# One-head TensorE loop body with branch arms, and query projections with x as the stationary column, in a decode-attention kernel

## The chip, the cores and the metric

The kernel runs on one core of one Trainium2 chip. The metric is the device time of one execution in microseconds (us); lower is better. "Before" was run beside every experiment on the same chip; its medians lie between 1328.2 and 1328.3 us throughout.

## The reference

Two attention layers for one new token, A and B, each with its own inputs; the two results are put side by side.

```python
# A: 32 heads, 32768 keys each        B: 32 query heads on 8 K/V heads, last 4096 keys
q = (x @ wq).reshape(B, Sq, H, Dh).transpose(0, 2, 1, 3)        # x is (1, 1, 512), Dh = 128
scores = jnp.einsum("bhqd,bhkd->bhqk", q, k_cache) * (Dh ** -0.5)
p = softmax(scores)
o = jnp.einsum("bhqk,bhkd->bhqd", p, v_cache)
out = o.transpose(0, 2, 1, 3).reshape(B, Sq, H * Dh) @ wo
```

All of it is bf16. There is one query, so each byte of K and V is used once: A alone reads 32 heads of 8 MB of K and 8 MB of V.

## The kernel before

Every operation is recorded first, with its dependencies; then each engine's list is emitted, with semaphore waits. TensorE and VectorE emit the A heads as a hardware loop, since their instructions repeat. The synchronizing engine (SP) issues the loads. K arrives with keys on the partitions, so TensorE transposes it (256 transposes of 128x128 a head), VectorE copies each eight of them from PSUM, and then the score matmuls run.

K has a buffer of three thirds, each half a head. Even heads lie in thirds 1 and 0, odd heads in 1 and 2. So the second half's addresses differ between even and odd heads, and the loop body holds two heads:

```python
def k_thirds(self, g):
    return (1, 0) if g % 2 == 0 else (1, 2)
...
for g in range(NQH):                                   # the A heads
    self.loop = {"pe": g // 2, "dve": g // 2}          # two heads are one iteration
    self.load_k(g, 1 if g < NQH - 1 else 2)            # 8 MB; waits until both thirds are free
    self.load_v(g)                                     # 8 MB; waits for the last value product
    self.emit_qcopy(g)
    self.emit_unit("A", g)                             # transposes, copies, scores
    self.emit_stats("A", g)
    self.emit_PT("A", g)
    self.emit_PV("A", g)                               # value product: 64 matmuls of 512 columns
...
with e.Fori(0, nit):
    for o, w in zip(its[-1], plans[-1]):
        run(e, o, [(sems[name], rel) for name, rel in w])
    for name, sem in sems.items():
        e.sem_inc(sem, -step[name])._wait_ge(sem, step[name])
```

The query projection uses each 128x128 block of wq as the stationary operand and one column of x as the moving one:

```python
for tt in range(4):
    for h in range(NQH):
        inst = e.matmul(ps[:, h:h + 1], lhsT=wq[:, 4096 * tt + 128 * h:4096 * tt + 128 * h + 128],
                        rhs=t["x"][:, tt:tt + 1], start=(tt == 0 and h == 0), stop=(tt == 3),
                        skip_group_check=True)
```

Of the kernel before, what the change touches and what calls it, by code (L numbers as in the profile page):

```python
# [9 lines left out]
DH = 128  # L10
NQH = 32
# [24 lines left out]
class Op:  # L36
# [2 lines left out]



    __slots__ = ("eng", "fn", "deps", "loop", "pos", "to", "users", "before")

    def __init__(self, eng, fn, deps, to, loop):
        self.eng = eng
        self.fn = fn
        self.deps = [d for d in deps if d is not None]
        self.to = to
        self.loop = loop
        self.users = []  # L50


class _Kernel:
# [30 lines left out]



    def op(self, eng, fn, *deps, to=None):
        o = Op(eng, fn, deps, to, self.loop.get(eng))
        self.prog[eng].append(o)
        return o  # L90

# [80 lines left out]
    def emit(self, eng):  # L172
        ops = self.prog[eng]
        nit = len({o.loop for o in ops} - {None})
        its = [[o for o in ops if o.loop == k] for k in range(nit)]
        first = next((i for i, o in enumerate(ops) if o.loop is not None), len(ops))
        pre, post = ops[:first], ops[first + sum(map(len, its)):]

        def run(e, o, waits):
            for sem, val in waits:  # L180
                e.wait_ge(sem, val)
            inst = o.fn(e)
            if o.to:
                inst.then_inc(self.sem(eng, o.to), 1)

        def straight(e, part, seen, base):
            for o in part:
                waits = []
                for name, (sem, val) in self.needs(o).items():
                    if val > seen.get(name, 0):  # L190
                        seen[name] = val
                        waits.append((sem, val - base.get(name, 0)))
                run(e, o, waits)

        def body(e):
            seen, base = {}, {}
            straight(e, pre, seen, base)
            if not nit:
                return

            assert len(set(map(len, its))) == 1
            need = [[self.needs(o) for o in it] for it in its]
            top = lambda k, name: max(n[name][1] for n in need[k] if name in n)
            sems = {name: sem for it in need[-2:] for n in it for name, (sem, _) in n.items()}
            step = {name: top(-1, name) - top(-2, name) for name in sems}
            for name in [x for x in sems if not step[x]]:
                if top(0, name) > seen.get(name, 0):
                    e.wait_ge(sems[name], top(0, name))
                    seen[name] = top(0, name)
                del sems[name]  # L210
            start = {name: top(-2, name) - step[name] * (nit - 1) for name in sems}
            plans = []
            for k, it in enumerate(need):
                cur, plan = {}, []
                for n in it:
                    w = []
                    for name, (sem, val) in n.items():
                        if name not in sems:
                            continue
                        rel = val - start[name] - step[name] * k  # L220
                        if rel > cur.get(name, 0):
                            cur[name] = rel
                            w.append((name, rel))
                    plan.append(sorted(w))
                plans.append(plan)
            for k, plan in enumerate(plans):
                for p, q in zip(plan, plans[-1]):
                    assert p == q or (k == 0 and set(p) <= set(q)), (eng, k, p, q)
            for name, sem in sems.items():
                if start[name] > 0:  # L230
                    e.sem_inc(sem, -start[name])._wait_ge(sem, start[name])
                elif start[name] < 0:
                    e.sem_inc(sem, -start[name])
            with e.Fori(0, nit):
                for o, w in zip(its[-1], plans[-1]):
                    run(e, o, [(sems[name], rel) for name, rel in w])
                for name, sem in sems.items():
                    e.sem_inc(sem, -step[name])._wait_ge(sem, step[name])
            for name in sems:
                base[name] = seen[name] = start[name] + step[name] * nit  # L240
            straight(e, post, seen, base)

        return body

    def alloc(self):
# [19 lines left out]
        for name, d in self.X.items():  # L265
            HG = d["HG"]
            self.c[name] = dict(
                x=sb(f"x_{name}", [128, 4], BF16),
                oc=[sb(f"oc_{name}{i}", [128, DH + 1], F32) for i in range(2)],
                b=sb(f"b_{name}", [128, 32], F32),  # L270
                cm=sb(f"cm_{name}", [128, 32], F32),
                mr=sb(f"mr_{name}", [1, HG], F32),
# [8 lines left out]

        self.qz = sb("qz", [128, 32 * self.X["B"]["NKVH"] + 64], BF16)
        self.qa = sb("qa", [128, NQH], BF16)
        self.qw = sb("qw", [128, 64], BF16)
        self.hw = sb("hw", [128, 32], F32)
        ps = nc.alloc_psum_tensor
# [38 lines left out]

    def k_thirds(self, g):
        return (1, 0) if g % 2 == 0 else (1, 2)

    def load_k(self, g, parts):
        w = HALF * DH  # L330
# [36 lines left out]
    def plan(self):  # L367
# [4 lines left out]
        self.copies = []  # L372
        self.pending = []
        self.psread = self.ptread = self.sread = self.accread = None
        self.gath = self.qcopy = self.hcopy = None
        self.constants()
        a, b = self.X["A"], self.X["B"]

# [15 lines left out]
        self.emit_spread("B")  # L394

        for g in range(NQH):
            self.loop = {"pe": g // 2, "dve": g // 2}
            self.load_k(g, 1 if g < NQH - 1 else 2)
            self.load_v(g)
            self.emit_qcopy(g)  # L400
# [17 lines left out]
    def constants(self):  # L418
# [15 lines left out]
        self.k_hw = pool(lambda g: g.memset(self.hw[:, :], 0.0))  # L434
        dve = lambda fn, *deps, **k: self.op("dve", fn, *deps, **k)
        dve(lambda v: v.memset(self.G[:, :], 0.0))
        self.accread = dve(lambda v: v.memset(self.ACC[:, :], 0.0))
        for n in ("B", "A"):
            self.op("act", lambda e, n=n: e.dma_start(
# [18 lines left out]
                             self.k_pool)  # L458

    def emit_qproj(self, name):  # L460
        t = self.c[name]
        slot = self.WQ_SLOT[name]
        ps, wq = self.ACC, self.vbuf[:, HALF * DH * slot:HALF * DH * (slot + 1)]
        def mm(e):
            inst = None
            for tt in range(4):
                for h in range(NQH):
                    inst = e.matmul(ps[:, h:h + 1], lhsT=wq[:, 4096 * tt + 128 * h:4096 * tt + 128 * h + 128],
                                    rhs=t["x"][:, tt:tt + 1], start=(tt == 0 and h == 0), stop=(tt == 3),
                                    skip_group_check=True)  # L470
            return inst
        o = self.op("pe", mm, (self.xsem[name], 16), self.landed("v", slot), self.accread, to="dve")
        self.free["v"][slot] = o
        if name == "B":
            o = self.op("dve", lambda v: v.tensor_copy(
                self.qz[:, 32:].rearrange("p (k w) -> p k w", w=32)[:, 0:8, 0:4],
                ps[:, 0:NQH].rearrange("p (k a) -> p k a", a=4)), o, self.k_pool)
            self.qb = o
        else:
            o = self.op("dve", lambda v: v.tensor_copy(self.qa[:, :], ps[:, 0:NQH]), o)  # L480
            self.qready = o
        self.accread = o

    def emit_qcopy(self, g):
        self.qcopy = self.op("act", lambda s: s.activation(
# [2 lines left out]
    def emit_unit(self, name, g, hooks={}):  # L488
# [4 lines left out]
        order = [(t, i, 8 * (t - lo) + st) for i, t in enumerate(thirds) for st in range(8)]  # L493
        for n, (t, i, st) in enumerate(order):
            for half in range(2):
                self.emit_T(HALF * lo + 16 * st + 8 * half, self.landed("k", g if name == "B" else i), t)
            if n % 2:
                if n // 2 in hooks:
                    hooks[n // 2]()
# [1 line left out]
                if len(self.pending) > 1:  # L501
                    self.emit_S(self.pending.pop(0))

    def emit_T(self, tile, landed, third):
        b = self.nbatch
        self.nbatch += 1
        T, KT = self.T[b % NT][:, :].bitcast(BF16), self.kt[b % NKT]
        src = self.kbuf[:, DH * tile:DH * tile + 1024]
        def tr(e):
            inst = None  # L510
            for k in range(8):
                inst = e.transpose(T[:, 128 * k:128 * k + 128], src[:, DH * k:DH * k + DH], self.ident[:, :])  # L512
            return inst
        o = self.op("pe", tr, landed, self.copies[b - NT] if b >= NT else self.k_ident, to="dve")
        self.copies.append(self.op("dve", lambda v: v.tensor_copy(KT[:, :], T[:, :]), o, to="pe"))  # L515
        self.free["k"][third] = o

# [24 lines left out]
    def emit_stats(self, name, g):  # L542
# [2 lines left out]
        d, t = self.X[name], self.c[name]  # L545
        KC, HG = d["KC"], d["HG"]
        W = KC * HG
        k = g % 2
        tr, m4 = self.tr, self.m4
        dve = lambda fn, *deps, **k: self.op("dve", fn, *deps, **k)  # L550
        o = dve(lambda v: v.reduce_max(tr["in"][:, 0:1], self.S[:, :], axis=AXX), self.sdone, self.k_pool,  # L551
# [1 line left out]
        if name == "A":  # L553
# [7 lines left out]
            o = dve(lambda v: v.tensor_copy(t["nb"][:, k:k + 1], self.ACC[:, 64:65]), o, to="act")  # L561
            self.sread = self.op("act", lambda s: s.activation(  # L562
                out=self.psb[:, :], in_=self.S[:, :], func=ACTF.Exp, bias=t["nb"][:, k:k + 1], scale=self.SCALE,
                accum_out=t["oc"][k][:, DH:DH + 1]), o, self.psread, to="pe")
            return
        o = dve(lambda v: v.transpose(tr["a"][:, :], tr["in"][:, :]), o)
        for c in range(STRIPS):
# [27 lines left out]
    def emit_PV(self, name, g):  # L595
# [23 lines left out]
            self.free["v"][i] = pv  # L619

        pv = self.emit_gather(name, g, DH, DH + 1)
        oc = t["oc"][g % 2][:, 0:DH]
        o = None
        for j in range(4):
            src, hot = acc[:, DH * j:DH * j + DH], t["hot"][:, j:j + 1]
# [11 lines left out]
    def emit_gather(self, name, g, c, c2):  # L637
# [1 line left out]
        t, HG, c0 = self.c[name], self.X[name]["HG"], self.GCOL[name]  # L639
        win = self.hw[:, :] if name == "A" else t["hsel"][:, 32 - HG * g:64 - HG * g]  # L640
        return self.op("pe", lambda e: e.matmul(  # L641
            self.G[0:32, c0 + c:c0 + c2], lhsT=win, rhs=t["oc"][g % 2][:, c:c2], start=False, stop=True,
            skip_group_check=True), self.accread, self.sread, self.hcopy if name == "A" else self.k_sel, to="dve")

    def emit_spread(self, name):
# [79 lines left out]
```

## Time and profile before

| | before |
|---|---|
| time, median of 6 runs | 1328.32 us (1328.13 to 1328.79) |
| DMA, 100 to 1280 us | all 16 engines busy, 433 GB/s |
| TensorE / VectorE busy | 73% / 57% |
| TensorE's wait for K | 156.2 us in 31 waits, 5.0 us each |
| one A head | 38.50 us (mean of heads 5 to 30, between first transposes) |
| TensorE words in the loop body | 1,579, by count in the program |

From the page of the kernel before: busy time by engine, the DMA share and rate in 40 slices of the span, and the data and instruction queues (packets, megabytes, share of the 16 engines' time).

```profile
span 1326.3 us, 28821 instructions
PE 972.0 (73%) x13436; PEld 681.1 (51%) x13436; DVE 749.4 (57%) x1345; ACT 54.8 (4%) x167; POOL 2.3 (0%) x17
...
DMA  9999999999999999999999999999999999999998
GB/s 403 440 425 428 436 437 431 435 433 433 433 425 439 437 433 429 441 431 427 439 433 427 439 441 429 427 441 433 425 439 439 429 431 441 429 429 439 433 427 349
...
q1 hardware_dynamic: 13048, 570.44, 99.6%
q8 instruction: 12, 0.20, 0.1%
```

The DMA engines are at 9 in every slice but the last. A 9 means only "90% or more", so it is worth asking for a stretch by itself. The windows view of the kernel before gives for 100 to 1280 us: busy time of PE, PEld, DVE, ACT and POOL, then the granted clock, the DMA share and GB/s.

```profile
100.00:1280.00 1180.00, 881.21 (x12045) 615.12 (x12043) 676.40 (x1186) 49.16 (x155) 0.00 (x0) 0.83 1.00 433
```

DMA share 1.00 at 433 GB/s; over the whole span the page has 570.43 MB read from HBM, 430 GB/s.

How much room is there behind the DMA? The timeline of the kernel before, cut to one head: an SPq line is the issue of a load, the PE line the first transposes of the next head, with the idle time before them and what ended it.

```profile
250.26 0.33 SPq L303 DMA_DIRECT2D kbuf<-in_A_k_cache_dram  x1
...
271.80 0.33 SPq L303 DMA_DIRECT2D vbuf<-in_A_v_cache_dram  x1
...
277.83 5.34 PE L512 MATMUL psT<-ident,kbuf 128*128 128x128 bf16 x64 [4.01 <-DMA kbuf<-in_A_k_cache_dram]
```

V is issued at 271.80 us, 6 us before the K ahead of it has landed, so the engines always have the next load in the queue. And TensorE itself idles for K in each head. A slower TensorE thus has two cushions: its own wait, and the depth of the queue.

The projections in the timeline of the kernel before (start, length):

```profile
13.35 3.58 PE L468 MATMUL psACC<-x_B,vbuf 128*128 128x1 bf16 x128 [13.35 <-DMA x_B<-in_B_x_dram]
16.96 0.19 DVE L475 CAST qz<-psACC 128x32 bf16<-128x32 f32 x1 [11.50 <-PE psACC L468]
...
35.21 3.35 PE L468 MATMUL psACC<-x_A,vbuf 128*128 128x1 bf16 x128
...
38.60 0.19 DVE L480 CAST qa<-psACC 128x32 bf16<-128x32 f32 x1 [2.69 <-PE psACC L468]
```

### The profile page before, as it was taken

What the parts mean: (1) busy time and instruction counts of PE and PEld (TensorE: products, weight loads), DVE (VectorE), ACT (ScalarE), POOL (GpSimd) and SP (SyncE); (2) the same over time, 40 slices, a digit from 0 to 9 for tenths busy, and PEclk for the clock granted to TensorE, in tenths of its full rate; (3) what the DMA queues carried; (4) which work ended last, traced back from release to release, by engine and by line L of the source; (5) the groups of instructions that cost most, each with busy time, mean ns of one, the idle gap of its engine ahead of it and who ended that gap; (6) DMA issues with size and microseconds to landing.
All of it is one profiled execution on the core that took longest, in us unless ns stands there. A gap on an engine that the chain in (4) does not pass through costs nothing.

```text
span 1326.3 us, 28821 instructions
## 1 busy us (share of the span) xinstructions
PE 972.0 (73%) x13436; PEld 681.1 (51%) x13436; DVE 749.4 (57%) x1345; ACT 54.8 (4%) x167; POOL 2.3 (0%) x17
## 2 busy tenths in 40 slices
PE   3757678787677878767787866778786677878686
PEld 3544446554444655444465544446554444655453
DVE  3655456664555666455566645556664555666473
ACT  0000000000000000000000000000000000000000
POOL 0000000000000000000000000000000000000000
PEclk9767788887878888787888878788887878888798
DMA  9999999999999999999999999999999999999998
GB/s 403 440 425 428 436 437 431 435 433 433 433 425 439 437 433 429 441 431 427 439 433 427 439 441 429 427 441 433 425 439 439 429 431 441 429 429 439 433 427 349
DMA packets 13351, 570.66 MB, mean 430 GB/s; under 512 B 1812, under 2 KB 1816, under 8 KB 2200
## 3 DMA queue, kind: packets, MB, share of 16 engines
q1 hardware_dynamic: 13048, 570.44, 99.6%
q8 instruction: 12, 0.20, 0.1%
q10 hardware_dynamic: 288, 0.00, 0.0%
q14 instruction: 3, 0.02, 0.0%
HBM read 570.43 MB, written 0.00 MB: 430 GB/s over the span
## 4 chain that ended last, share of the span: by engine, by line
DMA 70%; PE 27%; DVE 1%; issue 0%; SPq 0%; ACT 0%
DMA kbuf<-in_A_k_cache_dram 65%; PE psT L512 23%; PE psS L534 4%; DMA kbuf<-in_B_k_cache_dram 3%; DMA kbuf<-in_A_wo_dram 3%; DVE kt L515 1%; PE psACC L614 0%; SPq L303 0%; DVE oc_A L630 0%; ACT psb L562 0%; DVE tr_in L551 0%; PE psPT L586 0%; ACT ptsb L589 0%; PE psPT L676 0%; PE psG L641 0%
## 5 line engine op out<-in xcount | busy, mean ns | idle before, releaser
L515 DVE COPY kt<-psT 128x1024 bf16<-128x1024 bf16 x1056 | 654.7, 684 | 236.3 <-PE psT L512 234.9
L512 PE MATMUL psT<-ident,kbuf 128*128 128x128 bf16 x8448 | 578.7, 234 | 167.5 <-DMA kbuf<-in_A_k_cache_dram 156.2
L512 PEld LDWEIGHTS psT<-ident,kbuf 128*128 128x128 bf16 x8448 | 539.2, 106 | 259.7 <-DMA kbuf<-in_A_k_cache_dram 164.3
L614 PE MATMUL psACC<-vbuf,ptsb 128*4 128x512 bf16 (+1 forms) x2112 | 190.4, 539 | 23.2 <-ACT ptsb L589 21.3
L534 PE MATMUL psS<-kt,qw 128*32 128x512 bf16 x2048 | 157.7, 385 | 15.5 <-DVE kt L515 15.5
L628 DVE TENSOR_SCALAR oc_A<-psACC,hot_A 128x128 f32<-128x128 f32 x32 | 11.2, 351 | 255.7 <-PE psG L641 255.7
L614 PEld LDWEIGHTS psACC<-vbuf,ptsb 128*4 128x4 bf16 (+1 forms) x2112 | 61.4, 113 | 142.7 <-issue 98.3
L562 ACT ACTIVATE psb<-psS,nb_A 128x512 bf16<-128x512 f32 x32 | 22.0, 687 | 1167.7 <-DVE nb_A L561 1167.7
L534 PEld LDWEIGHTS psS<-kt,qw 128*32 128x32 bf16 x2048 | 34.1, 95 | 58.0 <-DVE kt L515 31.4
L641 PE MATMUL psG<-oc_A,hw 128*32 128x128 f32 (+1 forms) x128 | 19.3, 227 | 52.3 <-DVE oc_A L630 52.3
L641 PEld LDWEIGHTS psG<-oc_A,hw 128*32 128x32 f32 x128 | 11.4, 109 | 62.4 <-DVE oc_A L630 55.0
L586 PE MATMUL psPT<-ident,psb 128*128 128x128 bf16 x136 | 18.4, 280 | 34.1 <-ACT psb L562 34.1
L630 DVE SCALAR_TENSOR_TENSOR oc_A<-psACC,hot_A,oc_A 128x128 f32<-128x128 f32 x96 | 33.7, 351 | 3.4
L551 DVE TENSOR_REDUCE tr_in<-psS 128x1 f32<-128x512 f32 x34 | 23.5, 692 | 17.3 <-PE psS L534 17.3
L586 PEld LDWEIGHTS psPT<-ident,psb 128*128 128x128 bf16 x136 | 10.4, 120 | 37.1 <-ACT psb L562 36.7
L555 PE MATMUL psACC<-rows,tr_in 128*1 128x64 f32 x64 | 8.7, 218 | 25.5 <-DVE tr_in L551 25.5
L589 ACT ACTIVATE ptsb<-psPT 128x512 bf16<-128x512 bf16 x34 | 20.3, 597 | 30.2 <-PE psPT L586 30.2
L555 PEld LDWEIGHTS psACC<-rows,tr_in 128*1 128x1 f32 x64 | 2.7, 81 | 35.1 <-DVE tr_in L551 35.1
L559 PE MATMUL psACC<-mr_A,nscale 1*128 1x1 f32 x64 | 12.1, 256 | 9.8 <-DVE mr_A L558 9.8
L559 PEld LDWEIGHTS psACC<-mr_A,nscale 1*128 1x128 f32 x64 | 9.4, 183 | 15.8 <-DVE mr_A L558 15.8
L561 DVE COPY nb_A<-psACC 128x1 f32<-128x1 f32 x32 | 5.1, 159 | 15.1 <-PE psACC L559 15.1
L558 DVE TENSOR_REDUCE mr_A<-psACC 1x1 f32<-1x64 f32 x32 | 6.8, 212 | 11.7 <-PE psACC L555 11.7
(71 smaller groups left out, 75.5 us busy)
## 6 DMA issues: line engine op xcount, KB each, us to landing
kbuf<-in_B_k_cache_dram SPq DMA_DIRECT2D x2, 4096.0 KB, 32.6
vbuf<-in_B_v_cache_dram SPq DMA_DIRECT2D x2, 4096.0 KB, 23.8
kbuf<-in_A_k_cache_dram SPq DMA_DIRECT2D x2, 4096.0 KB, 22.3
vbuf<-in_B_wq_dram SPq DMA_DIRECT2D x1, 4096.0 KB, 12.4
vbuf<-in_A_wq_dram SPq DMA_DIRECT2D x1, 4096.0 KB, 32.2
kbuf<-in_B_wo_dram SPq DMA_DIRECT2D x2, 2048.0 KB, 33.5
kbuf<-in_A_wo_dram SPq DMA_DIRECT2D x1, 1408.0 KB, 28.9
kbuf<-in_A_wo_dram SPq DMA_DIRECT2D x1, 1024.0 KB, 31.0
```

The lines of the kernel that those rows point to most:

```text
L512: inst = e.transpose(T[:, 128 * k:128 * k + 128], src[:, DH * k:DH * k + DH], self.ident[:, :])
L515: self.copies.append(self.op("dve", lambda v: v.tensor_copy(KT[:, :], T[:, :]), o, to="pe"))
L534: inst = e.matmul(self.S[32 * c:32 * c + 32, :], lhsT=win, rhs=self.kt[(bb + c // 2) % NKT][:, 512 * (c % 2):512 * (c % 2) + 512], start=b ...
L551: o = dve(lambda v: v.reduce_max(tr["in"][:, 0:1], self.S[:, :], axis=AXX), self.sdone, self.k_pool, to="pe" if name == "A" else None)
L555: o = self.op("pe", lambda e: e.matmul(self.ACC[0:1, 0:64], lhsT=tr["in"][:, 0:1], rhs=self.rows64[:, :], start=True, stop=True, skip_grou ...
L559: o = self.op("pe", lambda e: e.matmul(self.ACC[:, 64:65], lhsT=self.nscale[:, :], rhs=t["mr"][0:1, :], start=True, stop=True, skip_group_ ...
L562: self.sread = self.op("act", lambda s: s.activation(out=self.psb[:, :], in_=self.S[:, :], func=ACTF.Exp, bias=t["nb"][:, k:k + 1], scale= ...
L586: inst = e.transpose(PT[:, 128 * jj:128 * jj + 128], self.psb[:, 128 * jj:128 * jj + 128], self.ident[:, :])
L589: self.ptread = self.op("act", lambda s: s.activation(out=self.ptsb[:, :], in_=PT[:, 0:512], func=ACTF.Copy), self.psread, to="pe")
L614: inst = e.matmul(acc[32 * c:32 * c + rows, 0:512], lhsT=lhsT, rhs=rhs, start=begin, stop=end, tile_position=(0, 32 * c), skip_group_check ...
L630: o = self.op("dve", lambda v, src=src, hot=hot: v.scalar_tensor_tensor(out=oc, in0=src, scalar=hot, in1=oc, op0=ALU.mult, op1=ALU.add), p ...
L641: return self.op("pe", lambda e: e.matmul(self.G[0:32, c0 + c:c0 + c2], lhsT=win, rhs=t["oc"][g % 2][:, c:c2], start=False, stop=True, ski ...
```

## The change

Its intent: a shorter TensorE program, with one head as the loop body. What differs between even and odd heads, the addresses of the second half's transposes, goes into the two arms of a branch, four times a head. With only one accumulator left for A, the exponential also waits for the head before. The projections use x as the stationary column, 32 matmuls of 512 columns in four column strips in place of 128 of one column; the rows are then copied and turned by 8 small matmuls.

```diff
... (cut: how the loop's operations are grouped)
+            odd = None
+            if any(two for two, _ in groups):
+                assert nit % 2 == 0
+                odd = e.alloc_register(f"{eng}_odd")
+                e.reg_mov(odd, 0)
             with e.Fori(0, nit):
-                for o, w in zip(its[-1], plans[-1]):
-                    run(e, o, [(sems[name], rel) for name, rel in w])
+                for two, part in groups:
+                    if two:
+                        with e.If_eq(odd, 0):
+                            for o, w in part:
+                                run(e, o, w, o.alts[0])
+                        with e.Else():
+                            for o, w in part:
+                                run(e, o, w, o.alts[1])
+                    else:
+                        for o, w in part:
+                            run(e, o, w)
+                if odd is not None:
+                    e.reg_sub(odd, 1, odd)
                 for name, sem in sems.items():
                     e.sem_inc(sem, -step[name])._wait_ge(sem, step[name])
... (cut)
-            self.loop = {"pe": g // 2, "dve": g // 2}
+            self.loop = {"pe": g, "dve": g // 2}
... (cut: emit_qproj)
-                for h in range(NQH):
-                    inst = e.matmul(ps[:, h:h + 1], lhsT=wq[:, 4096 * tt + 128 * h:4096 * tt + 128 * h + 128],
-                                    rhs=t["x"][:, tt:tt + 1], start=(tt == 0 and h == 0), stop=(tt == 3),
-                                    skip_group_check=True)
+                for b in range(2):
+                    for c in range(STRIPS):
+                        w = 4096 * tt + 512 * (4 * b + c)
+                        inst = e.matmul(banks[b][32 * c:32 * c + 1, :], lhsT=t["x"][:, tt:tt + 1], rhs=wq[:, w:w + 512],
+                                        start=(tt == 0), stop=(tt == 3), tile_position=(0, 32 * c), skip_group_check=True)
... (cut)
+        for b in range(2):
+            o = self.op("dve", lambda v, b=b: v.tensor_copy(self.qrow[:, 512 * b:512 * b + 512], banks[b][:, :]), o)
... (cut)
+            for b in range(2):
+                for i in range(4):
+                    inst = e.matmul(ps[:, 16 * b + i:16 * b + i + 13:4], lhsT=self.qrow[:, 512 * b + 128 * i:512 * b + 128 * i + 128],
+                                    rhs=self.ident[:, 0:97:32], start=True, stop=True, skip_group_check=True)
... (cut: emit_unit)
+                if name == "A" and i == 1:
+                    alts = [HALF * min(self.k_thirds(x)) + 8 * (16 * self.last_half(x) + 2 * (st % 8) + half) for x in (0, 1)]
... (cut: A's exponential)
-                accum_out=t["oc"][k][:, DH:DH + 1]), o, self.psread, to="pe")
+                accum_out=t["oc"][k][:, DH:DH + 1]), o, self.psread, self.gath if g else None, to="pe")
```

More of the change, by code (lines that the diff above doesn't have):

```diff
@@ L36, with __init__ @@
 class Op:
-    __slots__ = ("eng", "fn", "deps", "loop", "pos", "to", "users", "before")
-    def __init__(self, eng, fn, deps, to, loop):
+    __slots__ = ("eng", "fn", "deps", "loop", "pos", "to", "users", "before", "alts")
+    def __init__(self, eng, fn, deps, to, loop, alts=None):
+        self.alts = alts
         self.eng = eng
@@ L83, in __init__, with op @@
         self.loop = {}
-    def op(self, eng, fn, *deps, to=None):
-        o = Op(eng, fn, deps, to, self.loop.get(eng))
+    def op(self, eng, fn, *deps, to=None, alts=None):
+        o = Op(eng, fn, deps, to, self.loop.get(eng), alts)
         self.prog[eng].append(o)
@@ L177, in emit, with run @@
         pre, post = ops[:first], ops[first + sum(map(len, its)):]
-        def run(e, o, waits):
+        def run(e, o, waits, fn=None):
             for sem, val in waits:
                 e.wait_ge(sem, val)
-            inst = o.fn(e)
+            inst = (fn or o.fn)(e)
             if o.to:
@@ L233, in body @@
                     e.sem_inc(sem, -start[name])
-            with e.Fori(0, nit):
-                for o, w in zip(its[-1], plans[-1]):
-                    run(e, o, [(sems[name], rel) for name, rel in w])
+            groups = []
+            for o, w in zip(its[-1], plans[-1]):
+                if not (groups and groups[-1][0] and o.alts):
+                    groups.append((bool(o.alts), []))
+                groups[-1][1].append((o, [(sems[name], rel) for name, rel in w]))
+            odd = None
[3 more added lines that the diff above has]
+                e.reg_mov(odd, 0)
+            with e.Fori(0, nit):
+                for two, part in groups:
[11 more added lines that the diff above has]
+                    e.reg_sub(odd, 1, odd)
                 for name, sem in sems.items():
@@ L268, in alloc @@
                 x=sb(f"x_{name}", [128, 4], BF16),
-                oc=[sb(f"oc_{name}{i}", [128, DH + 1], F32) for i in range(2)],
+                oc=[sb(f"oc_{name}{i}", [128, DH + 1], F32) for i in range(2 if name == "B" else 1)],
                 b=sb(f"b_{name}", [128, 32], F32),
@@ L283, in alloc @@
         self.qa = sb("qa", [128, NQH], BF16)
+        self.qrow = sb("qrow", [128, 1024], BF16)
         self.qw = sb("qw", [128, 64], BF16)
@@ L327, in k_thirds, with last_half @@
         return (1, 0) if g % 2 == 0 else (1, 2)
+    def last_half(self, g):
+        t = self.k_thirds(g)
+        return t[1] - min(t)
     def load_k(self, g, parts):
@@ L374, in plan @@
         self.psread = self.ptread = self.sread = self.accread = None
-        self.gath = self.qcopy = self.hcopy = None
+        self.gath = self.qcopy = self.hcopy = self.qread = None
         self.constants()
@@ L436, in constants @@
         dve(lambda v: v.memset(self.G[:, :], 0.0))
+        dve(lambda v: v.memset(self.PT[:, :], 0.0))
         self.accread = dve(lambda v: v.memset(self.ACC[:, :], 0.0))
@@ L462, in emit_qproj @@
         slot = self.WQ_SLOT[name]
-        ps, wq = self.ACC, self.vbuf[:, HALF * DH * slot:HALF * DH * (slot + 1)]
+        wq = self.vbuf[:, HALF * DH * slot:HALF * DH * (slot + 1)]
+        banks = (self.ACC, self.PT)
         def mm(e):
@@ L466, in mm, with turn @@
             for tt in range(4):
-                for h in range(NQH):
-                    inst = e.matmul(ps[:, h:h + 1], lhsT=wq[:, 4096 * tt + 128 * h:4096 * tt + 128 * h + 128],
-                                    rhs=t["x"][:, tt:tt + 1], start=(tt == 0 and h == 0), stop=(tt == 3),
-                                    skip_group_check=True)
+                for b in range(2):
[3 more added lines that the diff above has]
+                                        start=(tt == 0), stop=(tt == 3), tile_position=(0, 32 * c), skip_group_check=True)
             return inst
-        o = self.op("pe", mm, (self.xsem[name], 16), self.landed("v", slot), self.accread, to="dve")
+        o = self.op("pe", mm, (self.xsem[name], 16), self.landed("v", slot), self.accread, self.qread, to="dve")
         self.free["v"][slot] = o
+        for b in range(2):
+            o = self.op("dve", lambda v, b=b: v.tensor_copy(self.qrow[:, 512 * b:512 * b + 512], banks[b][:, :]), o)
+        self.accread = o
+        ps = self.G[:, 400:432]
+        def turn(e):
+            inst = None
+            for b in range(2):
+                for i in range(4):
+                    inst = e.matmul(ps[:, 16 * b + i:16 * b + i + 13:4], lhsT=self.qrow[:, 512 * b + 128 * i:512 * b + 128 * i + 128],
+                                    rhs=self.ident[:, 0:97:32], start=True, stop=True, skip_group_check=True)
+            return inst
+        o = self.op("pe", turn, o, self.qread, self.k_ident, to="dve")
         if name == "B":
@@ L476, in emit_qproj @@
                 self.qz[:, 32:].rearrange("p (k w) -> p k w", w=32)[:, 0:8, 0:4],
-                ps[:, 0:NQH].rearrange("p (k a) -> p k a", a=4)), o, self.k_pool)
+                ps.rearrange("p (k a) -> p k a", a=4)), o, self.k_pool)
             self.qb = o
         else:
-            o = self.op("dve", lambda v: v.tensor_copy(self.qa[:, :], ps[:, 0:NQH]), o)
+            o = self.op("dve", lambda v: v.tensor_copy(self.qa[:, :], ps), o)
             self.qready = o
-        self.accread = o
+        self.qread = o
     def emit_qcopy(self, g):
@@ L495, in emit_unit @@
             for half in range(2):
-                self.emit_T(HALF * lo + 16 * st + 8 * half, self.landed("k", g if name == "B" else i), t)
+                tile = 16 * st + 8 * half
+                alts = None
+                if name == "A" and i == 1:
+                    alts = [HALF * min(self.k_thirds(x)) + 8 * (16 * self.last_half(x) + 2 * (st % 8) + half) for x in (0, 1)]
+                    assert alts[g % 2] == HALF * lo + tile
+                self.emit_T(HALF * lo + tile, self.landed("k", g if name == "B" else i), t, alts)
             if n % 2:
@@ L502, in emit_unit, with emit_T @@
                     self.emit_S(self.pending.pop(0))
-    def emit_T(self, tile, landed, third):
+    def emit_T(self, tile, landed, third, alts=None):
         b = self.nbatch
@@ L507, in emit_T, with tr @@
         T, KT = self.T[b % NT][:, :].bitcast(BF16), self.kt[b % NKT]
-        src = self.kbuf[:, DH * tile:DH * tile + 1024]
-        def tr(e):
+        def tr(e, tile=tile):
+            src = self.kbuf[:, DH * tile:DH * tile + 1024]
             inst = None
@@ L513, in tr @@
             return inst
-        o = self.op("pe", tr, landed, self.copies[b - NT] if b >= NT else self.k_ident, to="dve")
+        o = self.op("pe", tr, landed, self.copies[b - NT] if b >= NT else self.k_ident, to="dve",
+                    alts=[lambda e, x=x: tr(e, x) for x in alts] if alts else None)
         self.copies.append(self.op("dve", lambda v: v.tensor_copy(KT[:, :], T[:, :]), o, to="pe"))
@@ L547, in emit_stats @@
         W = KC * HG
-        k = g % 2
+        k = g % len(t["oc"])
         tr, m4 = self.tr, self.m4
@@ L621, in emit_PV @@
         pv = self.emit_gather(name, g, DH, DH + 1)
-        oc = t["oc"][g % 2][:, 0:DH]
+        oc = t["oc"][g % len(t["oc"])][:, 0:DH]
         o = None
@@ L641, in emit_gather @@
         return self.op("pe", lambda e: e.matmul(
-            self.G[0:32, c0 + c:c0 + c2], lhsT=win, rhs=t["oc"][g % 2][:, c:c2], start=False, stop=True,
+            self.G[0:32, c0 + c:c0 + c2], lhsT=win, rhs=t["oc"][g % len(t["oc"])][:, c:c2], start=False, stop=True,
             skip_group_check=True), self.accread, self.sread, self.hcopy if name == "A" else self.k_sel, to="dve")
```

## The prediction

> **What bounds the kernel now.** The page's slices show the 16 DMA engines at 90% or more of every slice until the last, moving 430 GB/s on average. The kernel reads 570.43 MB, and at 430 GB/s that alone is 1326.6 us, the whole span (1326.3 us). TensorE is busy 73%, VectorE 57%. The chain of waits gives TensorE transposes 23%, but during those pieces earlier loads were still running: the timeline shows loads of K and V issued about 6 to 10 us before the load ahead of them lands (K issued at 250.26 us, the V ahead landing at 258.42; V issued at 271.80, K landing at 277.78). So the engines never run dry. Per head (38.7 us) TensorE itself waits about 5 us for K (the table of waits: 156.2 us in 31 waits). So a slower TensorE has two cushions of about 5 us.
>
> **What the change does, costed.**
> 1. Query projections: 128 one-column matmuls took 3.58 us (B) and 3.35 us (A). They become 32 matmuls of 512 columns in four strips; 32 such in the B value product took 1.90 to 3.59 us, so the same again. Added: two 128x512 copies (a like-sized copy of the output took 0.69 us) and 8 tiny matmuls, an estimated 0.5 us. Each projection ends about 2 us later. B's result is needed only after K lands at 23.8 us (it was ready at 17.2). A's delay moves the first B statistics (39.27 to 42.59 us) up to about K's landing at 43.55: at most 0.5 us for TensorE, nothing for the DMA.
> 2. Loop body: one head in place of two. Per head four compare-and-branch and four jumps. [...]most of it under the 0.42 us waits for VectorE's copies that stand before each transposing batch. The one remaining accumulator of A is free some 20 us before the next exponential: no wait.
> 3. Instruction fetch: the queue of instructions shows 12 packets, 0.20 MB, for the whole run, about TensorE's program once; so the present body, some 1,600 words or six 16 KB blocks by my count, ran 16 times without a refetch. [...]The new body is about 1,060 words, the program about 2,230 against 3,100: I expect 8 or 9 packets. Three packets fewer are worth 0.1 to 0.2 us of the DMA.
>
> **On the critical path:** almost nothing. The same bytes move through full engines.
>
> **Prediction:** 1328.2 us, range 1325.0 to 1332.0. Faster by over 2%: 0.01; within 2%: 0.98; slower by over 2%: 0.01.
>
> **What would show it right:** DMA slices all 9 again, about 430 GB/s; heads still 38.7 us apart; TensorE's wait for K about 5 us, perhaps 0.3 to 0.7 us shorter; 8 or 9 instruction packets; the projection's matmuls 2 to 4 us and qz/qa about 2 us later than before.
>
> **What would make it wrong:** the branch arms making the sequencer refetch blocks in each iteration (instruction packets in the hundreds). A fetch queued behind data could stall TensorE over 10 us in a head (the 1 KB load of x took 12.0 us to land); that would use up both cushions: K waits gone, slices below 9.

The forecast's sum came to 1328.2 us: the 1328.32 us of the kernel before less 0.1 to 0.2 us for three instruction packets, with all that TensorE gains or loses counted as hidden. Two passages are cut from it where marked: the author's figure for the branches in the loop's term, and a remark on instruction fetch; no trace or run of this case shows either. "Most of it" in the second item is the time of these branches. The term entered the sum as hidden.

## More of the kernel before

Over heads 5 to 30, from the trace's issue and landing times, V goes out 6.7 us before the load ahead lands (least 6.0), K 8.3 us before (least 7.6).

## The result

The changed kernel took 1328.22 us (median of 6 runs, 1327.29 to 1329.88), before 1328.32 us; the ratio is 1.000, with a 95% interval of 0.9987 to 1.0013. Here and below a ratio is the mean time of one kernel's fast runs over that of the other's of the same rounds, so it is not quite the ratio of the medians quoted. The result is correct.

The page of the changed kernel, the same lines:

```profile
span 1326.0 us, 28874 instructions
PE 967.7 (73%) x13260; PEld 676.0 (51%) x13260; DVE 753.0 (57%) x1350; ACT 54.8 (4%) x167; POOL 2.2 (0%) x17
...
DMA  9999999999999999999999999999999999999998
GB/s 403 445 420 427 427 431 439 437 427 435 441 427 433 435 433 433 433 437 429 435 437 429 435 435 433 431 435 437 429 433 435 435 433 433 433 431 435 435 433 351
...
q1 hardware_dynamic: 13048, 570.44, 99.7%
q8 instruction: 9, 0.15, 0.0%
```

Its windows view for 100 to 1280 us:

```profile
100.00:1280.00 1180.00, 878.51 (x12039) 613.54 (x12036) 677.06 (x1186) 49.17 (x155) 0.00 (x0) 0.83 1.00 433
```

The same bytes, the same rate, engines full. Three instruction packets fewer are all that changed on the DMA. (The chain of waits of this page could be followed over only 3 per cent of the span, so it is not read here.)

The table of waits, first of the kernel before, then of the changed one (who waited for whom: us in total, times, longest):

```profile
PE psT L512 <- DMA kbuf<-in_A_k_cache_dram: 156.2, 31, 11.4
```

```profile
PE psT L560 <- DMA kbuf<-in_A_k_cache_dram: 157.4, 31, 12.5
...
PE psT L560 <- issue: 2.4, 1, 2.4
```

TensorE waits as long for K as before. New is one wait of 2.4 us for "issue", that is, for nothing that the profile shows. The timeline of the changed kernel puts it into the first head, and shows the projections:

```profile
13.48 0.59 PE L500 MATMUL psACC<-vbuf,x_B 128*1 128x512 bf16 x4 [13.48 <-DMA x_B<-in_B_x_dram]
...
16.42 0.56 PE L500 MATMUL psPT<-vbuf,x_B 128*1 128x512 bf16 x4
17.04 0.69 DVE L506 CAST qrow<-psACC 128x512 bf16<-128x512 f32 x1 [11.29 <-PE psPT L500]
17.76 0.69 DVE L506 CAST qrow<-psPT 128x512 bf16<-128x512 f32 x1
...
18.51 0.37 PE L513 MATMUL psG<-ident,qrow 128*128 128x4 bf16 x8 [1.53 <-DVE qrow L506]
18.92 0.19 DVE L518 CAST qz<-psG 128x32 bf16<-128x32 f32 x1 [0.46 <-PE psG L513]
...
37.48 0.19 DVE L523 CAST qa<-psG 128x32 bf16<-128x32 f32 x1 [0.46 <-PE psG L513]
...
104.60 2.70 PE L560 MATMUL psT<-ident,kbuf 128*128 128x128 bf16 x31 [2.40 <-issue]
...
118.02 0.33 SPq L326 DMA_DIRECT2D vbuf<-in_A_v_cache_dram  x1
...
121.67 5.37 PE L560 MATMUL psT<-ident,kbuf 128*128 128x128 bf16 x64 [1.64 <-DMA kbuf<-in_A_k_cache_dram]
```

B's query is ready at 19.11 us in place of 17.15. The matmuls themselves took as long as the 128 before (3.5 us); the copies and the turning are the 2 us. In the first head the stall and its follow-on made the V load go out at 118.02 us in place of 114.97, which is still 3.6 us before the K ahead of it landed (121.62). A packet of instructions was read from 102.25 to 103.32 us by the trace's DMA records, inside the stall. It happens once in the run.

One head takes 38.57 us (before 38.50; mean of heads 5 to 30).

### The profile page after: what moved, and what is told of

Its sections match the earlier page's. It is cut to its first block, busy times and chain, and to the rows that moved or that the text cites. A ratio compares the mean times of both kernels' runs of the same rounds, so it can differ in the third digit from the quotient of the medians.

```text
span 1326.0 us, 28874 instructions
## 1 busy us (share of the span) xinstructions
PE 967.7 (73%) x13260; PEld 676.0 (51%) x13260; DVE 753.0 (57%) x1350; ACT 54.8 (4%) x167; POOL 2.2 (0%) x17
## 5 line engine op out<-in xcount | busy, mean ns | idle before, releaser
L560 PE MATMUL psT<-ident,kbuf 128*128 128x128 bf16 x8448 | 579.9, 234 | 170.2 <-DMA kbuf<-in_A_k_cache_dram 157.4
L663 PE MATMUL psACC<-vbuf,ptsb 128*4 128x512 bf16 (+1 forms) x2112 | 187.5, 532 | 22.8 <-ACT ptsb L638 22.0
L583 PEld LDWEIGHTS psS<-kt,qw 128*32 128x32 bf16 x2048 | 34.1, 95 | 57.4 <-DVE kt L564 30.4
L607 DVE TENSOR_REDUCE mr_A<-psACC 1x1 f32<-1x64 f32 x32 | 6.8, 212 | 11.7 <-PE psACC L604 11.7
```

The source lines that it names most:

```text
L560: inst = e.transpose(T[:, 128 * k:128 * k + 128], src[:, DH * k:DH * k + DH], self.ident[:, :])
L583: inst = e.matmul(self.S[32 * c:32 * c + 32, :], lhsT=win, rhs=self.kt[(bb + c // 2) % NKT][:, 512 * (c % 2):512 * (c % 2) + 512], start=b ...
L663: inst = e.matmul(acc[32 * c:32 * c + rows, 0:512], lhsT=lhsT, rhs=rhs, start=begin, stop=end, tile_position=(0, 32 * c), skip_group_check ...
```

## The experiments

The theory after the result: **hidden**. The DMA engines are full, and nothing that the change did to TensorE is larger than the two cushions. A rival: the two halves of the change **cancel**, the projection gaining a few us, the arms costing as much. And a question that "no difference" leaves open: what does the new loop cost or gain where nothing hides it?

| run | TensorE words in the body, by count | instruction packets | median us | ratio to before (95%) | DMA share and GB/s, 100 to 1280 us |
|---|---|---|---|---|---|
| before | 1,579 | 12 | 1328.3 | | 1.00, 433 |
| changed | 1,064 | 9 | 1328.22 | 1.000 (0.9987 to 1.0013) | 1.00, 433 |
| proj_only | 1,579 | 11 | 1328.06 | 0.9999 (0.9985 to 1.0012) | 1.00, 433 |
| loop_only | 1,064 | 10 | 1329.21 | 1.0009 (0.9996 to 1.0023) | 1.00, 433 |
| after_pv2 | 1,192 | 9 | 1344.81 | 1.012 (1.0103 to 1.0137) | 1.00, 427 |
| after_pv3 | 1,320 | 10 | 1409.77 | 1.0616 (1.0598 to 1.0634) | 0.96, 408 |
| body4 | 3,151 | 116 | 1350.93 | 1.0173 (1.0156 to 1.019) | 1.00, 427 |
| before_pv15 | 1,707 | 147 | 1373.85 | 1.0338 (1.0321 to 1.0355) | 0.99, 419 |
| before_pv2 | 1,835 | 148 | 1400.65 | 1.0531 (1.0508 to 1.0553) | 0.96, 410 |
| before_pv3 | 2,091 | 164 | 1502.63 | 1.131 (1.1291 to 1.1328) | 0.90, 381 |
| light_before | 1,579 | 12 | 1134.55 | 0.8537 (0.8524 to 0.855) | |
| light_noarms | 793 | 7 | 1158.55 | 0.8725 (0.871 to 0.8739) | |
| light_after | 1,064 | 9 | 1189.09 | 0.8955 (0.8942 to 0.8969) | |
| light_arms2 | 1,850 | 148 | 1254.71 | 0.9447 (0.9431 to 0.9463) | |

Every matmul is counted as two words (weight load and matmul; the page of the kernel before has 13,436 of each); the count is of the compiled program, with both arms. The DMA share is time with packets under way: in after_pv2 and body4 it reads 1.00 while the rate is 427 GB/s, so read it with the rate beside it.

### proj_only and loop_only: each half alone

```diff
  # proj_only: the kernel before with the changed emit_qproj, and its qrow tile and zeroed psPT bank
  # loop_only: the changed kernel with the emit_qproj of before
```

> The kernel before with the new query projection alone. Theory H (hidden: the DMA engines are full, so neither part reaches the time): ratio within 0.999 to 1.001, the first B load of V issued within 2 us of 30.2 us, DMA slices all 9. Rival C (the two parts cancel, the projection gains and the arms cost): 1 to 5 us faster than before.

> The changed kernel with the old projection, so the loop body of one head with branch arms alone. H: ratio within 0.999 to 1.001; instruction packets 10 or 11 (one block more than the changed kernel's 9); one stall of TensorE of about 2.4 us with nothing to wait for in the first head, as in the changed kernel. Rival C: 1 to 5 us slower than before.

Neither half moves the time: 0.9999 and 1.0009, both intervals across 1. The projection's packets come to 11, the loop's to 10. The loop alone has the one stall (2.71 us in its first head), the projection alone has none; its first load of B's V went out at 29.16 us, as expected. Cancelling is excluded as far as these intervals go, about 0.2 per cent or 3 us; a cancelling of 1 to 3 us, the lower end of the rival, would fit into them. The traces narrow it: the data packets fill 1321.5 us of each engine's time in before and in proj_only, 1322.1 us in loop_only and in the changed kernel, and of the span only 3.1 to 4.1 us in the four are not packet time. So in the profiled runs neither half gained or cost more than about 1 us, and "hidden" stands.

### light_before, light_after: the same pair where the DMA does not hide TensorE

```diff
-            self.load(self.kbuf[:, w * lo:w * lo + 2 * w], src, self.mark("k", 0), *free)
+            cut = w // 4 if g >= 2 else w
+            both = lambda a: a.rearrange("p (t x) -> p t x", t=2)[:, :, 0:cut]
+            self.load(both(self.kbuf[:, w * lo:w * lo + 2 * w]), both(src), self.mark("k", 0), *free)
...
-        self.load(self.vbuf[:, :], self.kv_src("v", "A", g)[:, 0, :], self.mark("v", 0), *self.free["v"])
+        self.load(self.vbuf[:, 0:8192], self.kv_src("v", "A", g)[:, 0, 0:8192], self.mark("v", 0), *self.free["v"])
```

> Wrong result on purpose: from the third A head on only a quarter of each K load, and of every A head's V load a quarter. This takes the DMA off the critical path, so that TensorE and VectorE set the pace and the cost of loop and arms shows. H: faster than before by 8 to 14 per cent (a head takes about 34 us in place of 38.7), waits for K near nothing from the fourth head on.

> The same cut of loads in the changed kernel; its time less that of light_before is what the change costs where nothing hides it. H in its mild form: the branches lie under the waits for VectorE's copies, so the heads are as long within 0.1 us and the whole within 5 us of light_before. [...]If arms cause refetches in every head: over 60 us longer, and over 50 instruction packets.

The results are wrong on purpose; all engines' instructions are the same. light_before takes 1134.55 us, a little faster than expected (14.6 per cent in place of 8 to 14, a head 32.4 us in place of 34); light_after takes 1189.09 us. With the DMA out of the way (share 0.32 to 0.34) **the changed kernel is 54.5 us slower**, 1.7 us a head. The mild form of the expectation (within 5 us) was too small, and there is no refetching (9 packets). Where does it come from? Means of heads 5 to 30, from the traces, in us:

| part of a head | light_before | light_noarms | light_after |
|---|---|---|---|
| gap before the first transpose | 0.33 | 0.72 | 0.93 |
| first 64 transposes | 3.82 | 4.40 | 4.49 |
| other 192 transposes, with score matmuls among them | 14.63 | 14.63 | 14.63 |
| last scores to value product | 5.89 | 5.88 | 5.87 |
| value product | 5.68 | 5.78 | 6.14 |
| value product's end to the gap | 2.07 | 2.07 | 2.07 |
| one head | 32.43 | 33.48 | 34.14 |

The third row has the branches, and takes 14.63 us with and without them. TensorE's weight loads still wait there for VectorE's copies, about 0.4 us each time, so a branch may be hidden under such a wait, as the prediction had it; what a branch costs by itself is not shown. The gap is the loop's end. The timelines show it: in light_before every second head is entered without a gap, the others after the loop's end (PEq, TensorE's sequencer); in light_after every head is entered through it. The tables of waits of light_before, light_noarms and light_after count it: 0.73 us each time without arms, 0.93 us with them. The first and the fourth line are the waits for VectorE's copies in light_before and light_after.

```profile
PEld psT L514 <- DVE kt L517: 69.9, 165, 0.4
PE psT L514 <- PEq L238: 10.9, 15, 0.7
```

```profile
PE psT L562 <- PEq L260: 22.5, 31, 0.8
```

```profile
PEld psT L562 <- DVE kt L566: 76.3, 180, 0.4
...
PE psT L562 <- PEq L260: 28.9, 31, 1.0
```

From the timelines, light_before and then light_after:

```profile
604.86 3.82 PE L514 MATMUL psT<-ident,kbuf 128*128 128x128 bf16 x64 [0.74 <-PEq L238]
...
637.39 3.82 PE L514 MATMUL psT<-ident,kbuf 128*128 128x128 bf16 x64
```

```profile
629.53 3.82 PE L562 MATMUL psT<-ident,kbuf 128*128 128x128 bf16 x64 [0.94 <-PEq L260]
...
663.28 5.16 PE L562 MATMUL psT<-ident,kbuf 128*128 128x128 bf16 x64 [0.92 <-PEq L260]
```

The gap explains 0.6 of the 1.7 us. The rest are the same matmuls at a slower clock: the same 64 transposes take 3.82 us in one head and 5.16 in the next. The windows views for 300 to 1050 us, light_before and then light_after (the granted clock is the third number from the end):

```profile
300.00:1050.00 750.00, 619.40 (x9120) 419.89 (x9120) 500.38 (x901) 37.25 (x117) 0.00 (x0) 0.92 0.34 129
```

```profile
300.00:1050.00 750.00, 617.57 (x8703) 419.69 (x8700) 480.08 (x858) 34.91 (x110) 0.00 (x0) 0.87 0.32 123
```

0.92 against 0.87. The clock records of the traces hold only 1.0 and 0.5, in stretches of 3.41 us or multiples of it (but for the last, which the end cuts off). In light_after one at 0.5 lasts from 662.9 to 666.3 us, on the slow transposes shown: over these 64 the mean is 0.71, over the fast ones 1.00. With the records cut into pieces of 3.41 us: in light_after, between 150 and 1000 us, TensorE (matmuls and weight loads) was busy for a median of 45 per cent of the 3.41 us before a piece at 0.5, and for a median of 100 per cent of those before one at 1.0; in the kernel before and in the changed one, counted the same way, it is 35 and 36 per cent against 100. Pieces at 0.5 come 1.5 times a head in light_before, 2.2 times in light_noarms and 2.4 times in light_after. The slow transposes come in fixed patterns too (every second head in light_after, two of five in light_noarms, none in light_before). So in these traces the lower clock comes after stretches in which TensorE was less busy. But no run changes the clock by itself, so that the extra gap is what lowers it is argued, not shown.

### light_arms2 and light_noarms: arms or loop end?

light_arms2 keeps two heads in the body and puts the even heads' second half into arms that are alike, with light loads and the old projection. light_noarms has one head in the body and no arms; all heads use thirds 1 and 0.

```diff
  # light_arms2
-            self.loop = {"pe": g, "dve": g // 2}
+            self.loop = {"pe": g // 2, "dve": g // 2}
...
-                if name == "A" and i == 1:
-                    alts = [ ... for x in (0, 1)]
+                if name == "A" and i == 1 and g % 2 == 0:
+                    alts = [HALF * lo + tile] * 2
  # light_noarms
-        return (1, 0) if g % 2 == 0 else (1, 2)
+        return (1, 0)
...
-                if name == "A" and i == 1:
+                if False:
```

> Light loads, old projection, two heads in the body as before, and the branch arms (both alike) round the second half of the even heads: arms without the loop of one head. If the arms are free and all of the 54 us between light_before and light_after comes of ending the loop once a head instead of once in two: 1132 to 1140 us, as light_before (1134.6). If the arms carry a share: half of that share over light_before, so up to 1160 us.

> Light loads, wrong result on purpose: one head in TensorE's loop body as in the changed kernel, but without arms, since all heads use the same two thirds of the K buffer (the quarter loads land well before the next head). If the arms are free and ending the loop once a head is the whole of the cost between light_before (1134.6 us) and light_after (1189.1 us): 1178 to 1192 us. If the arms are the cost: 1130 to 1142 us. 9 instruction packets or fewer in either case; if the K waits are not near nothing, it tells nothing.

light_arms2 missed both expectations: 1254.71 us, with 148 instruction packets. Its body of 1,850 words was fetched anew in each iteration, so it tells nothing of the arms. It does tell of the fetch (below).

light_noarms took 1158.55 us, between its two expectations. Its first head began 11.8 us earlier than light_after's (70.95 against 82.71 us, as its first K load is a quarter too), so heads have to be compared, as the table does: 33.48 us. Of the 1.71 us a head between light_before and light_after, 1.05 us come with the loop end once a head and no arms, 0.66 us with the arms. In idle time that is 0.39 and 0.21 us; the remainder are the slower transposes and value products. The arms' 0.21 us lie in the gap at the loop's end, where the register that tells odd from even is changed (that it is this instruction was not tested), not in the branches among the transposes. The expectation that the arms would be free failed by these 0.66 us.

### after_pv2 and after_pv3: how deep are the cushions?

```diff
                     for kc in range(16) for c in range(STRIPS)]
+            todo = 2 * todo          # after_pv3, before_pv3: 3 * todo
             rows = 4
```

The value product is done again over itself; the result stays correct.

> The changed kernel with each A head's value product done twice (same result), 64 more matmuls a head, an estimated 3.5 to 5 us of TensorE. Theory H (TensorE has about 5 us of waiting for K in each head, and the next load is issued about 6 us before the one ahead lands): 38.0 us or less of work against 38.6 us a head, so the ratio stays within 0.995 to 1.01, with waits for K about 1 us or less. A theory that TensorE's chain of 27 to 30 per cent lies on the path: at least 100 us longer.

> The value product three times. H: both cushions are spent, a head takes about 34.1 + 2 x 3.5 = 41 us, so 1400 to 1420 us; waits for K gone; DMA slices at 8 or below.

The 3.5 to 5 us for 64 more matmuls are the author's estimate; in the trace of the kernel before, 32 such matmuls of B took 1.90 us, and 64 of A 4.93 to 6.36 us in the heads looked at. after_pv2's value product takes 3.26 us more (8.98 against 5.72 us a head), and the time rises by 16.5 us in place of 104 (32 x 3.26). So about five sixths of the added work are hidden. But the expectation (ratio up to 1.01, waits for K of 1 us) was a little off: 1.012, and TensorE still waits.

```profile
PE psT L560 <- DMA kbuf<-in_A_k_cache_dram: 73.3, 26, 13.0
```

V now goes out 4.3 us before the load ahead lands (before 6.7). Already then DMA engines run dry now and then: 6.9 us of idle time per engine from 100 us to 8 us before the end, against 0.2 in the kernel before, and 411 of the 8,064 packets of 64 KB took over 2.5 us, against 55 in the changed kernel (the usual one takes 2.42); all data packets together take 9.6 us more of each engine's time than before. Most of these slow packets lie in the first 6 us after a V issue. Why they are slow is left open.

after_pv3 spends both cushions: 1409.77 us, K is waited for only once, before the first head (11.7 us), V goes out only 0.3 us before the load ahead lands, 40.96 us a head, where 34.1 + 7 = 41 was estimated. DMA slices at 8 or below were expected and did not come: nearly all are still 9, at a share of 0.96 and 408 GB/s.

### body4, before_pv3, before_pv2, before_pv15: the size of the body

```diff
  # body4, from the kernel before
-            self.loop = {"pe": g // 2, "dve": g // 2}
+            self.loop = {"pe": g // 4, "dve": g // 2}
  # before_pv15, from the kernel before (before_pv2 and before_pv3: 2 * todo, 3 * todo)
+            todo = todo[:32] + todo
```

> The kernel before with four heads in TensorE's loop body: 3,151 words by count, over twelve 16 KB blocks, against 1,579 before. If a body [...]is fetched anew in each of the 8 iterations[...]: about 100 instruction packets, 1.07 us each on one of 16 engines, so about 6 us longer (0.5 per cent), plus stalls at the jump back that the K wait hides. If bodies of any size stay: 17 packets and no change. If refetches stall TensorE beyond the cushion: over 1 per cent longer.

> The same tripling in the kernel before. If the loop of one head costs TensorE 1.7 us a head where nothing hides it, as the two runs with light loads say, this is 30 to 60 us faster than after_pv3 (a head about 39.5 us, 1355 to 1370 us). If that difference belonged to the light loads only, the two are alike within 10 us.

> The kernel before with the value product twice, as after_pv2 (1344.8 us). Its body is 1,835 words by count[...]: 12 to 15 instruction packets. If the loop of one head costs TensorE 1.7 us a head that only the cushions hide, the V loads go out earlier than in after_pv2 and this takes 1328 to 1338 us, at least 6 us less than after_pv2. If the loop's cost belonged to light loads only: 1342 to 1347 us.

> The kernel before with half of the value product done once more: 32 more matmuls a head, 1,707 words in the body by count. 1,579 words stayed (12 packets), 1,835 did not (148 packets, 1400.7 us). [...]1,707 words can still stay: 12 to 13 packets and 1328 to 1331 us, the cushions hiding 2 us more of work. If the border is [...]below: about 140 packets and over 1350 us.

body4 was expected to refetch, 6 us for it, and did: 116 packets. But it cost 22.6 us, the last case of its expectation. The packets take only 0.5 per cent of the engines. By the DMA records, each engine spends 6.6 us more on instruction packets than before, 10.0 us more on data packets (343 of the 8,064 took over 2.5 us, against 13 before), and 5.0 us more without a packet. TensorE also stalls at the jump back, as the lines show; that these stalls are the cause of the slow data packets is not shown. From body4's page, waits and timeline:

```profile
q8 instruction: 116, 1.90, 0.5%
```

```profile
PE psT L512 <- issue: 29.9, 4, 8.2
```

```profile
400.22 5.58 PE L512 MATMUL psT<-ident,kbuf 128*128 128x128 bf16 x64 [6.87 <-issue]
```

before_pv3 and before_pv2 were meant to compare the two loops under more TensorE work, and cannot: their bodies of 2,091 and 1,835 words are refetched too. I had counted on a border above 1,835 words, which no run had shown, and had not counted before_pv3's at all. before_pv15 then looked for the border, and with 1,707 words it is already beyond it. The page's line of instruction packets and the longest wait without a shown releaser, before_pv15:

```profile
q8 instruction: 147, 2.41, 0.6%
```

```profile
PE psT L512 <- issue: 95.0, 13, 8.9
```

So 1,579 words stay on the core for 16 iterations (12 packets in the whole run, none of them between 146 and 1317 us), 1,707 words do not (147 packets). Beyond the border the whole body comes anew, by the count: before_pv15 has 135 packets more than before in 15 jumps back, nine each, and 1,707 words fill about seven at some 250 words a packet (an estimate from about 3,100 words of program and 12 packets before, about 2,230 and 9 after). A refetched iteration costs about 3 us after what the cushions take: (1373.85 - 1328.19) / 15 = 3.0 us in before_pv15, (1350.93 - 1328.31) / 7 = 3.2 us in body4; the longest single stall was 9.9 us, in before_pv2. The 3.0 us take the added value product (1.7 us a head) for hidden, which was not tested at that size.

This is where the change is worth something. With the value product done twice, the kernel before takes 1400.65 us and the changed one 1344.81 us: the one-head body of 1,192 words is far from the border, the two-head body of 1,835 beyond it. The price of the loop end shows nowhere in that pair, and was not isolated there.

## Why the prediction was right

The predicted time was 1328.2 us and "within 2%"; measured 1328.22 us. Point by point:

- **What bounds the kernel**: right. DMA share 1.00 at 433 GB/s before and after; each half of the change alone leaves the time within 0.1 per cent.
- **Two cushions of about 5 us**: right in kind, and after_pv2 and after_pv3 show them. 3.26 us more of TensorE a head are mostly hidden; of the 7.3 us more in after_pv3, about a third shows (81.5 us of 32 x 7.3). The DMA's cushion gives out gradually: with 4.3 us of lead left, engines are already idle at times (6.9 us each in after_pv2).
- **Projections**: the 32 matmuls as estimated (3.5 us in B), the copies 0.69 us each, the 8 small matmuls 0.37 in place of 0.5 us. B's query is ready 1.96 us later, as predicted. A's was not "about 2 us later": from its first weight load to the finished copy it took 4.2 us in place of 3.6, and was done earlier (37.67 against 38.79 us) because it started earlier.
- **Loop, "most of it under the 0.42 us waits"**: this term, the author's estimate, was mis-sized. Where the DMA does not hide it, the loop costs 1.71 us a head. That the branches among the transposes would not be felt was right (14.63 us in each form); left out were the loop's end, now once a head, and the slower clock, which make up all of the 1.71 us. That so large a miss did not reach the time is owed to the width of the cushions, not to the estimate: for this term the right result was luck. What a branch among the transposes costs by itself no run shows; the loop's end, where the program also sets its semaphores back, leaves TensorE idle for 0.72 us in light_noarms and 0.93 us in light_after, which has the arms and their register.
- **"TensorE's wait for K … perhaps 0.3 to 0.7 us shorter"**: wrong; 157.4 against 156.2 us. The loop's end lies just where TensorE waits for K. That it is passed while K is on its way, so that the wait does not get shorter by it, fits both tables of waits but was not tested.
- **Instruction fetch**: 9 packets as predicted (8 or 9). Missed was that the first pass through the body stalls once, 2.4 us.
- **What would make it wrong**: refetching of blocks in each iteration. It did not happen in the changed kernel, but it did in body4 and before_pv15, which took 1.7 and 3.4 per cent longer.

No version with a correct result beats both kernels, and the profile says why: only the end of the span leaves the DMA idle. The last slice of 33 us moves 349 GB/s in place of 433, which is 33 x (1 - 349/433) = 6.4 us or 0.5 per cent.

## What to carry to other kernels

With the DMA engines full (share 1.00) and the next load always in the queue, little of the time given to or taken from the other engines was seen here (about a sixth of it in after_pv2); ask how deep the queue's lead is, and test a change with the loads cut if you want its own cost. Read GB/s beside the DMA share: body4 was 1.7 per cent slower at a share of 1.00. The hardware loop's body had a size limit here, between 1,579 and 1,707 words, that shows as instruction packets (12 at 1,579 words, 147 at 1,707): count words, and read the packets of the instruction queue before adding to a body. "The same time" can hide both a cost (here 1.7 us of TensorE a head) and a worth (here distance from the refetch border).
